# Attention and FFN in one kernel: heads in natural rows, three score buffers shared by two engines, score fills in twos

## Chip, cores, metric

One core of one Trainium2 chip. The metric is device time in microseconds of one execution. The profiled execution is one of a kernel's runs; its span is about 2 us shorter than the time that is reported for it. In the lines of profiles PE is TensorE, PEld its weight loads, DVE VectorE, ACT ScalarE and POOL GpSimd; x4 stands for four instructions merged into one line, and `<-PE ps` names what ended a wait.

## The reference

Batch 1, 2048 tokens, width 512, 32 heads of 16, FFN width 1792, bfloat16 inputs. The inputs' setup is left out.

```python
def reference(A_x, A_wqkv, A_wo, B_x, B_w1, B_w3, B_w2):
    x = A_x
    xn = _layernorm(x)                                   # no gain, no bias
    qkv = (xn @ A_wqkv).reshape(B, S, 3, 32, 16) ...     # q, k, v per head
    p = softmax(einsum("bhqd,bhkd->bhqk", q, k) * 0.25)
    a = einsum("bhqk,bhkd->bhqd", p, v) ... @ A_wo
    h = silu(xn @ B_w1) * (xn @ B_w3)
    return x + a + h @ B_w2
```

## The kernel before

The kernel is laid out ahead of time by a small scheduler in Python: it keeps a model clock for each engine, and at each step hands TensorE the next piece of work by priority. What runs on the chip is the fixed order of instructions that comes out, with semaphores between the engines. A "pair" below is one pair of PSUM banks with scores of two heads, 128 keys by 512 queries each. There are 1024 pairs. ScalarE turns a pair into exponentials with one instruction ("exp"); VectorE does it with "p1" on a pair and four further instructions for every two pairs, by integer arithmetic on bfloat16 bits. The weighted sums of V ("PV"), the FFN and the output projections are TensorE's other work; its last part of the FFN, h times w2, is called w2 here.

Scores use 32 rows of the array for each head, so a head's 16 numbers of K and Q are spread over the 16 even rows of their group by a DMA through a staging tile, and the rest is filled with a constant that adds the bias of the exponent:

```python
        def pack(dst, keys, dkeys, scale, halves=(0, 1)):
            def evac(bk, o, rel):
                def emit():                                  # PSUM -> stg on VectorE (scaled for Q)
                    ...
                    for hh in halves:
                        P.post("sp", lambda hh=hh: moves(hh), ready=q.end + _LAT, prio=1)
                def moves(hh):
                    m = P.dma(lambda e: e.dma_start(dst(hh), stg[64 * hh:64 * hh + 64, sl, :]), ...)
```

The constant is put there by ScalarE (first group) and by POOL (the others). The score buffers are private: banks 0–3 are two pairs for ScalarE, banks 4–5 one pair for VectorE. Scores for ScalarE go first:

```python
        def try_a():                      # a pair for ScalarE
            bufs = [0]
            if idle((2, 3)):
                bufs = [0, 1]
            ...
            x = score(2 * buf, "A", *nx)
        def try_d():                      # a pair for VectorE
            if st["pos"] >= NR or st["early"] or not idle((4, 5)) or dbuf[0] > P.t:
                return False
            x = score(4, "D", *nx)
        ...
                    elif try_a() or try_d() or (... try_dense() ... try_pv() ... try_dense()):
```

`early` is the prologue: as long as it lasts, banks 4–6 belong to the projections and VectorE gets no scores. All 16 copies of V for all heads, 512 columns each, lie in that phase.

## Time and profile before

| | before |
|---|---|
| time, median of the first 3 runs | 813.42 us (812.09 to 815.43) |
| span of the profiled run | 812.3 us |
| exps on ScalarE / p1 on VectorE | 794 / 230 |
| first exp, first p1 | 19.1 us, 48.9 us |
| 100th pair, 1000th pair begun | 105.0 us, 774.0 us |
| from the 1000th pair to the end | 38.3 us |

The last two rows cut the span into three lengths: a **head** (to the 100th pair: 105.0 us), a **middle** of 900 pairs (669.0 us) and a **rest** (38.3 us). A pair counts as begun when its exp or p1 starts; the times are read off the single records of the trace. Such marks are better than idle columns here, since the records of successive exps overlap.

ScalarE's timeline of the kernel before (start, length, engine, line, instruction, and in brackets the idle time ahead with what ended it):

```profile
7.67 1.09 ACT L1391 ACTIVATE f_xnT<-ps 128x512 bf16<-128x512 bf16 x2 [1.29 <-PE ps L1384]
10.56 1.09 ACT L1391 ACTIVATE f_xnT<-ps 128x512 bf16<-128x512 bf16 x2 [1.81 <-PE ps L1384]
14.01 0.60 ACT L1391 ACTIVATE f_xnT<-ps 128x512 bf16<-128x512 bf16 x1 [2.35 <-PE ps L1384]
18.12 1.09 ACT L1391 ACTIVATE f_xnT<-ps 128x512 bf16<-128x512 bf16 x2 [3.52 <-PE ps L1384]
19.10 1.95 ACT L1788 ACTIVATE f_PT<-ps 128x1024 bf16<-128x1024 f32 x2
```

ScalarE has waited 9 us in four gaps for transposed tokens by the time of its first exp, and the copies at 14.01 and 18.12 us are of later tokens than the first scores need.

### The profile page before, as it was taken

The numbers are of one execution on the slowest core, as the hardware profiler recorded it, in microseconds if no ns is written. First come the engines' busy times: TensorE is split into PE (matmuls) and PEld (weight loads), VectorE is DVE, ScalarE is ACT, GpSimd is POOL, SyncE is SP. The second block draws the span as 40 slices with busy tenths as digits, with TensorE's granted clock in tenths as the row PEclk, the third lists the DMA queues.
The fourth block names the chain that finished last, engine by engine and source line by source line (L and its number), as shares of the span: only waits on it lengthen the run. The fifth ranks groups of instructions, "written<-read, shape, count | busy, mean of one in ns | idle before, by whom it ended". The sixth has DMA issues, their size and how long they took to land.

```text
span 812.3 us, 20816 instructions
## 1 busy us (share of the span) xinstructions
PE 775.6 (95%) x8925; PEld 224.6 (28%) x8925; DVE 775.1 (95%) x1015; ACT 776.0 (96%) x874; POOL 44.1 (5%) x54
## 2 busy tenths in 40 slices
PE   6999999999999999999999999999999999999987
PEld 4332222222222222222222222222222222222222
DVE  8679999999999999999999999999999999999982
ACT  4899999999999999999999999999999999999992
POOL 4500100000000000000001000000000000000000
PEclk9999999999999999999999999999999999999997
DMA  5216333233222313333112434321223432222211
GB/s 182 54 31 149 49 49 52 45 54 40 29 22 41 49 38 43 41 54 47 19 25 28 60 41 54 48 33 40 18 27 55 67 34 34 49 27 22 28 9 31
DMA packets 88783, 36.96 MB, mean 45 GB/s; under 512 B 73193, under 2 KB 85097, under 8 KB 88681
## 3 DMA queue, kind: packets, MB, share of 16 engines
q1 hardware_dynamic: 88680, 35.53, 29.9%
q8 instruction: 72, 1.18, 0.6%
q14 instruction: 31, 0.25, 0.1%
HBM read 22.81 MB, written 2.10 MB: 31 GB/s over the span
## 4 chain that ended last, share of the span: by engine, by line
ACT 50%; PE 24%; DVE 19%; DMA 3%; issue 2%; POOL 1%; SPq 1%; DVEq 0%; POOLq 0%
ACT f_PT L1788 48%; PE ps L1356 9%; PE ps L1742 8%; DVE f_xd L1837 6%; PE ps L2010 6%; ACT f_th L1517 3%; DVE f_xd L1900 3%; DVE f_xd L1909 2%; DVE f_xd L1950 2%; DVE f_xd L1893 2%; DMA f_R<-f_Rrow 2%; DMA f_Rrow<-f_Rc 1%; DVE f_hT L1531 1%; SPq L2058 1%; DVE f_t L1521 1%
## 5 line engine op out<-in xcount | busy, mean ns | idle before, releaser
L1788 ACT ACTIVATE f_PT<-ps 128x1024 bf16<-128x1024 f32 x794 | 746.4, 1091 | 9.9 <-PE ps L1742 9.1
L1742 PE MATMUL ps<-f_QT,f_KT 32*128 32x512 bf16 x2048 | 331.0, 385 | 14.1 <-ACT f_PT L1788 7.1
L1837 DVE TENSOR_SCALAR f_xd<-ps 128x1024 int16<-128x1024 f32 x230 | 278.6, 1211 | 1.6 <-PE ps L1742 1.2
L2010 PE MATMUL ps<-f_PT,f_Vaug 128*17 128x512 bf16 (+1 forms) x1588 | 211.0, 386 | 0.3 <-DVE f_xd L1900 0.3
L2010 PE MATMUL ps<-f_xd,f_Vaug 128*17 128x512 bf16 (+1 forms) x1380 | 191.5, 387 | 3.5 <-DVE f_xd L1950 2.6
L1742 PEld LDWEIGHTS ps<-f_QT,f_KT 32*128 32x128 bf16 x2048 | 83.5, 91 | 328.6 <-ACT f_PT L1788 277.2
L1356 PE MATMUL ps<-f_xnT,f_w 128*32 128x512 bf16 x1792 | 145.0, 384 | 2.5 <-DVE f_hT L1531 0.9
L1900 DVE TENSOR_TENSOR f_xd<-f_xd 128x2048 bf16<-128x2048 bf16 x115 | 142.1, 1235 | 0.0
L1909 DVE TENSOR_SCALAR f_xd<-f_xd 128x2048 int16<-128x2048 int16 x115 | 81.2, 706 | 0.0
L1893 DVE TENSOR_SCALAR f_xd<-f_xd 128x2048 int16<-128x2048 int16 x115 | 79.4, 691 | 0.6 <-PE ps L1356 0.2
L1950 DVE TENSOR_SCALAR f_xd<-f_xd 128x2048 int16<-128x2048 int16 x115 | 79.0, 687 | 0.0
L1356 PE MATMUL ps<-f_w,f_hT 128*32 128x512 bf16 x896 | 74.9, 384 | 0.0
L2010 PEld LDWEIGHTS ps<-f_PT,f_Vaug 128*17 128x17 bf16 (+1 forms) x1588 | 50.6, 92 | 54.4 <-issue 44.7
L2010 PEld LDWEIGHTS ps<-f_xd,f_Vaug 128*17 128x17 bf16 (+1 forms) x1380 | 46.2, 92 | 54.7 <-issue 30.4
L2075 POOL TENSOR_TENSOR f_onorm<-f_U,f_R 128x512 bf16<-128x512 f32 x15 | 21.5, 1431 | 705.2 <-DMA f_R<-f_Rrow 549.3
L1356 PEld LDWEIGHTS ps<-f_xnT,f_w 128*32 128x32 bf16 x1792 | 36.6, 94 | 64.9 <-issue 56.5
L1517 ACT ACTIVATE f_th<-ps 128x512 f32<-128x512 f32 x56 | 38.7, 691 | 0.0
L1531 DVE SCALAR_TENSOR_TENSOR f_hT<-f_t,ps 128x512 bf16<-128x512 bf16 x56 | 37.8, 675 | 0.7 <-PE ps L1356 0.5
L1521 DVE SCALAR_TENSOR_TENSOR f_t<-f_th,ps 128x512 bf16<-128x512 f32 x56 | 37.7, 674 | 0.5 <-ACT f_th L1517 0.3
L1356 PEld LDWEIGHTS ps<-f_w,f_hT 128*32 128x32 bf16 x896 | 18.6, 94 | 26.8 <-issue 22.4
L1356 PE MATMUL ps<-f_wo,f_onorm 128*32 128x512 bf16 x272 | 22.2, 401 | 1.9 <-POOL f_onorm L2075 1.8
L2028 DVE COPY f_U<-ps 128x512 f32<-128x512 f32 x31 | 21.1, 679 | 0.4 <-PE ps L2010 0.3
(80 smaller groups left out, 240.6 us busy)
## 6 DMA issues: line engine op xcount, KB each, us to landing
f_w<-in_B_w_dram SPq DMA_DIRECT2D x112, 128.0 KB, 2.7
f_R<-f_Rrow SPq DMA_DIRECT2D x124, 32.0 KB, 4.4
f_xr<-in_A_x_dram SPq DMA_DIRECT2D x16, 128.0 KB, 3.8
out_dram<-f_xn_sb SPq DMA_DIRECT2D x16, 128.0 KB, 2.5
f_KT<-f_stg SPq DMA_DIRECT2D x31, 64.0 KB, 2.0
f_QT<-f_stg SPq DMA_DIRECT2D x31, 64.0 KB, 2.0
f_U<-f_U SPq DMA_DIRECT2D x60, 32.0 KB, 1.9
f_w<-in_B_w_dram SPq DMA_DIRECT2D x7, 256.0 KB
```

The source lines that it names most:

```text
L1356: ins = e.matmul(bank(bk)[32 * i:32 * i + 32, 0:ncols], make_lhsT(i), rhs_ap, start=start, stop=stop, tile_position=(0, 32 * i))
L1517: q = P.op("act", lambda e: e.activation(th[:, ss, :], bank(bk), ACTF.Tanh, scale=0.5), reads=[("ps", bk)], writes=[("th", ss)], dur=a_cos ...
L1521: q2 = P.op("dve", lambda e: e.scalar_tensor_tensor(t1[:, ss, :], th[:, ss, :], 1.0, bank(bk), ALU.add, ALU.mult), reads=[("th", ss), ("ps ...
L1531: q = P.op("dve", lambda e: e.scalar_tensor_tensor(hT[:, fc, :], t1[:, ss, :], 0.5, bank(bk), ALU.mult, ALU.mult), reads=[("t1", ss), ("ps ...
L1742: ins = e.matmul(bank(b), l_, r_, start=True, stop=True, tile_position=(rp, 0))
L1788: q = P.op("act", lambda e: e.activation(PT[:, s_, :], ps[:, b0 * 512:(b0 + 2) * 512], ACTF.Exp, scale=ASC, bias=ABIAS), reads=[("ps", b0) ...
L1837: q = P.op("dve", lambda e: e.tensor_scalar(dsl[:, ys, 1024 * c:1024 * c + 1024], ps[:, 4 * 512:6 * 512], G_LO, 32767.0, ALU.max, ALU.min) ...
L1893: P.op("dve", lambda e: e.tensor_scalar(dsl[:, NY + m_, 0:n], y, 0x7F, 0x3F00, ALU.bitwise_and, ALU.bitwise_or), reads=YK, writes=[("ds", ...
L1900: q_ = P.op("dve", lambda e: e.tensor_tensor(t_ap.bitcast(BF16), y.bitcast(BF16), t_ap.bitcast(BF16), ALU.mult), reads=YK + [("ds", NY + m ...
L1909: q_ = P.op("dve", lambda e: e.tensor_scalar(g_ap, y, -G_LO, 0.0, ALU.add, ALU.max), reads=YK, writes=[("g", g_, k) for k in range(n // 51 ...
L1950: q_ = P.op("dve", lambda e: e.tensor_scalar(y, y, 0x7F80, None, ALU.bitwise_and), reads=YK, writes=YK, dur=s_cost(n), name="e", lock=True)
L2010: ins = e.matmul(bank(PV)[32 * j:32 * j + (17 if g % 2 == 0 else 32), :], v_, p_, start=s0, stop=s1, tile_position=(0, 32 * j))
```

## The change

The intent: (1) K and Q stay in the rows in which the projection delivers them, two heads in each group of 32 rows; Q is kept in two copies, each masked to one of the two heads, so that the other head's 16 rows multiply by zero. Staging DMAs and constant fills go; the bias moves into p1. (2) The first projections are done token tile by token tile, with dummy matmuls put in to keep the array warm, and their copies are shared by ScalarE and VectorE; V for heads 0 to 7 is packed by fours into 4 copies, and the other 16 copies of V move out of the prologue. (3) The three pairs of score banks are shared by both engines; where two are free, TensorE fills both, on opposite row groups, before it turns to column work. (4) PV groups may wait longer for more members. The core of the diff (cut; "..." marks cuts, and the comments in it are added here):

```diff
-    NPR = 10
+    NPR = 12
-    PVQ = 20
+    PVQ = 28
+    A_SOON = 0.7
+    D_SOON = 0.6
+    VB0 = 24
+    VBS = 5
-    ABIAS = -127.0 * math.log(2.0) + math.log(KAPPA)
+    ABIAS = math.log(KAPPA)
...
-        def kt_fill(g):                       # POOL fills of K with the constant
...
@@ tile_QT
+                    q = P.op("dve", lambda e: e.tensor_scalar(QT[:, s1, :], bank(bk), QS, None, ALU.mult), ...)
+                    q = P.op("dve", lambda e: e.tensor_scalar(QT[:, s0, :], QT[:, s1, :], msk[:, 0:1], None, ALU.mult), ...)
+                    q = P.op("dve", lambda e: e.tensor_scalar(QT[:, s1, :], QT[:, s1, :], msk[:, 1:2], None, ALU.mult), ...)
...
+        for t in range(NT):                   # V of heads 8 to 31, out of the prologue
+            crit.append((VB0 + VBS * t, k, tile_VB(t)))
...
+        def open_bufs():
+            bs = [0]
+            if idle((2, 3)):
+                bs.append(1)
+            if not st["early"] and idle((4, 5)):
+                bs.append(2)
+            return [b_ for b_ in bs if pbuf[b_] <= P.t + A_EARLY]
 
         def try_a():
...
+            two = len(free) > 1
+            if not two and not st["early"]:   # one free buffer: fill it alone only when it is due
+                due = max(P.t, P.free["act"]) + 0.905 * st["wait_a"] - A_SOON
+                if due > P.t and sorted(pbuf)[1] <= due + A_OVER:
+                    return False
+            if not one_a(free[0], ...):
+                return False
+            if two and not st["early"]:
+                one_a(free[1], st["last_par"])
...
         def try_d():
-            if st["pos"] >= NR or st["early"] or not idle((4, 5)) or dbuf[0] > P.t:
+            if st["pos"] >= NR or st["early"] or st["hold_d"] or not d_due():
...
-                                                          G_LO, 32767.0, ALU.max, ALU.min),
+                                                          YB, G_LO, ALU.add, ALU.max),
...
-            if len(pick) < 4 and not closed and P.t - oldest < 1.2:
+            if len(pick) < 4 and not closed and P.t - oldest < 2:
...
-                    elif try_a() or try_d() or (...
+                    elif try_d() or try_a() or (...
```

## The prediction

> **What bounds the kernel now.** I read the page's busy shares first, then the same engines stage by stage, then the groups of instructions, then a few microseconds of the timeline, and last the start times of single records in the trace. Busy shares and stages:
>
> ```profile
> PE 775.6 (95%) x8925; PEld 224.6 (28%) x8925; DVE 775.1 (95%) x1015; ACT 776.0 (96%) x874; POOL 44.1 (5%) x54
> ...
> 0.00:20.00 20.00, 12.84 (x126) 8.54 (x126) 16.22 (x42) 8.91 (x13) 8.56 (x20) 1.00 0.58 184
> 20.00:40.00 20.00, 18.12 (x280) 7.83 (x284) 14.04 (x30) 17.64 (x24) 11.48 (x12) 1.00 0.24 55
> 40.00:60.00 20.00, 19.78 (x264) 6.40 (x256) 15.42 (x20) 18.27 (x21) 0.00 (x0) 1.00 0.11 27
> 60.00:780.00 720.00, 701.17 (x8026) 194.11 (x8024) 714.67 (x902) 715.36 (x802) 24.05 (x22) 1.00 0.31 43
> ```
>
> (columns of the stages: PE, weight load, DVE, ACT, POOL busy, clock, DMA share, GB/s.) From 60 to 780 us three engines are all over 97% busy. There are 1024 pairs of score banks; ScalarE turns 794 of them into exponentials (L1788), VectorE 230 (L1837 and a chain of four operations per two pairs). The pairs are dealt out between the two, so their joint rate sets the end, and TensorE fills the banks for both:
>
> ```profile
> L1788 ACT ACTIVATE f_PT<-ps 128x1024 bf16<-128x1024 f32 x794 | 746.4, 1091 | 9.9 <-PE ps L1742 9.1
> L1742 PE MATMUL ps<-f_QT,f_KT 32*128 32x512 bf16 x2048 | 331.0, 385 | 14.1 <-ACT f_PT L1788 7.1
> L1837 DVE TENSOR_SCALAR f_xd<-ps 128x1024 int16<-128x1024 f32 x230 | 278.6, 1211 | 1.6 <-PE ps L1742 1.2
> L1900 DVE TENSOR_TENSOR f_xd<-f_xd 128x2048 bf16<-128x2048 bf16 x115 | 142.1, 1235 | 0.0
> L1909 DVE TENSOR_SCALAR f_xd<-f_xd 128x2048 int16<-128x2048 int16 x115 | 81.2, 706 | 0.0
> ```
>
> The idle column suggests that almost nothing is lost (9.9 us on ScalarE). It misleads: records of successive exps overlap (mean 1091 ns), so a short wait is hidden in the overlap. Start to start in the trace, a fed exp takes 904 ns (half of them 904 or 905), but the 744 exps that start between 60 and 780 us average 930 ns: **19 us lost on ScalarE**. In 129 gaps with over 30 ns lost, 16.6 us together, nearly every exp starts 0.43 us after a score matmul starts: it waited for that matmul. The same count for VectorE (p1 1.134, multiply 1.133, the three others 0.60 each when fed) gives **17 us lost**, about 9 of it beside the 1.43 us normalisations on POOL (L2075).
>
> Why is TensorE late? The timeline:
>
> ```profile
> 401.77 0.12 PEld L1742 LDWEIGHTS ps<-f_QT,f_KT 32*128 32x128 bf16 x4 [0.42 <-ACT f_PT L1788]
> 401.78 0.41 PE L1742 MATMUL ps<-f_QT,f_KT 32*128 32x512 bf16 x4
> 402.12 0.10 PEld L2010 LDWEIGHTS ps<-f_PT,f_Vaug 128*32 128x32 bf16 x4 [0.23 <-issue]
> 402.12 0.40 PE L2010 MATMUL ps<-f_PT,f_Vaug 128*32 128x512 bf16 x4
> ...
> 402.45 0.10 PEld L1742 LDWEIGHTS ps<-f_QT,f_KT 32*128 32x128 bf16 x2 [0.23 <-ACT f_PT L1788]
> 402.45 0.39 PE L1742 MATMUL ps<-f_QT,f_KT 32*128 32x512 bf16 x2
> 402.77 0.12 PEld L1356 LDWEIGHTS ps<-f_w,f_hT 128*32 128x32 bf16 x8 [0.23 <-issue]
> 402.77 0.61 PE L1356 MATMUL ps<-f_w,f_hT 128*32 128x512 bf16 x8
> ```
>
> Score matmuls use 32 rows of the array ("row"), all others 32 columns ("col"). Row to col and col to row take 0.32 us start to start (medians 318 and 322 ns), col to col 0.216; a second pair on the other two row groups (the x4 at 401.78) costs almost nothing. Between 60 and 780 us I count 738 row stretches, 520 with one pair, 206 with two, 12 with three, and 1616 col groups, of which 166 PV groups hold two matmuls where four fit. The sum, 738 x 0.64 + 878 x 0.217 + 33 between row groups, is 695 us of 720: TensorE is truly full, though its score loads show 277 us of waits for ScalarE.
>
> **What the Trainium skill says.** "TensorEngine Tiling (Array Packing)", Key Properties: changing the tiling mode drains TensorE, while different tiles can run in parallel. The trace agrees: 0.32 against 0.216 us, and four row groups together. "SBUF — State Buffer", Who interferes with whom: a VectorE instruction in a 2-port mode and a GpSimd one lock each other out for a whole instruction. The trace agrees, and it costs the prologue dearly:
>
> ```profile
> 7.82 1.90 POOL L1275 TENSOR_SCALAR f_KT<-f_pat 128x2048 int16<-128x2048 int16 x1
> 7.88 2.30 DVE L1242 TENSOR_SCALAR f_xn_sb<-f_xd,f_mv,f_lnr 128x512 bf16<-128x512 bf16 x2 [0.59 <-POOL f_lnr L1230]
> ```
>
> Two such normalisations take 0.70 us elsewhere, 2.30 beside the POOL fill. "TensorE: Matmul & The Clock Gate", The HAM clock gate: cold matmuls of 128 columns run at about 107 ns, warm ones at 56, and idling makes it cold again. The 40 warming matmuls here took 4.45 us (111 each), and the first projections at 14.3 us still ran 0.43 us apart, twice the later 0.216. "VectorE: DVE Perf Modes", tier table: tensor_scalar on 16-bit SBUF data reaches 4x. The 2048-wide ones here take 0.60 us start to start, which agrees.
>
> **The change part by part.**
> *Row stretches.* Three buffers shared, two filled at once on opposite row groups. If the 966 pairs of the middle come in about 580 stretches rather than 738, TensorE saves 158 x (0.64 - 0.217) = 67 us. Fuller PV groups: some 80 groups fewer, 17 us. V for heads 8 to 31 moves from the prologue into the run: 64 groups, 14 us back. TensorE falls to about 86 to 90% of the middle: no longer a bound, but single fills stay whenever VectorE holds one of three buffers (p1 alone reads 1.13 us of each 3.2 us).
> *ScalarE in the middle.* It loses 19 us; I let it keep 6. (720 - 27 for 56 tanh - 6)/0.904 = 760 exps instead of 744.
> *VectorE in the middle.* A pair costs 1.134 + (1.133 + 3 x 0.60)/2 = 2.60 us; 222 pairs, 17 us lost, so 126 us of other work. Added: two mask multiplies for each of 15 Q tiles; between the 0.15 us that the 2048-wide rate gives and the 0.32 us of L1242, I estimate 0.25 each, 7.5 us. I let the losses fall from 17 to 12, as the POOL normalisations stay. (720 - 126 - 7.5 - 12)/2.60 = 221 pairs. Together 981 against 966 pairs, 1.6% more: **-11 us**.
> *The added YB, the bias and the missing clamp* leave element counts alike: 0. The staging DMAs that go were hidden: 0.
> *Prologue.* Now the first exp starts at 19.1 us, the first p1 at 48.9, and 35 + 5 pairs have begun by 60 us. The POOL fills of K (11 us, one on the path: 1.6) go; the first projections are done tile by tile on a warm array with evacuations on both engines, and the next transposes no longer stand in front of them. First exp, estimated: about 12 us. The early phase needs 4 V evacuations instead of 16 and no second K and Q tile, so it can end when VectorE has normalised all x tiles: 12 tiles at about 1.05 us, plus some 6 us of copies, from 11 us, is about 30. Pairs by 60 us: 14 exps before 30 (two in 2.5 us, as now), 32 after, 5 or 6 by VectorE beside 16 V copies of 0.46 us and the next K and Q: 52. Twelve ahead, at the present pace of 916 pairs in 680 us (0.74 us each): **-9 us**.
> *Tail.* The same structure: 0, with a doubt of 3 us (its clock halves at 789 us, 0.54 in the stage 790 to 800).
> Sum: 813.4 - 11 - 9 = about **794 us**.
>
> **The rivals.**
> *A: the losses do not move.* Sharing three buffers, VectorE takes one for the wait, the fill and p1, and ScalarE is back on two; the kernel fills a lone buffer only when the next exps are about 0.7 us off, little over 0.32 + 0.43. For it: the just-in-time rule; against: the freed array and the 40% of the time with three. ScalarE keeps 15 us, the middle gains 2 to 3, the time is 802 to 805.
> *B: VectorE starves instead.* Its buffer is now asked for only 0.6 us before it is free, where before it had its own. For it: p1 must follow in order; against: scores for VectorE go first and the chain offers other work. 5% of VectorE lost (36 us) is 10 to 14 pairs: about 800 to 803.
> *C: both engines run full and the prologue gains more* (first exp at 11, early phase over by 25 us): ScalarE loses 3 us, 16 pairs ahead at the start: 785 to 788.
> *D: the array goes cold in the middle, or the saturation test of the int16 conversion fails and the slow plan runs as well.* Nothing in the trace speaks for it: between 20 and 40 us, with PE 91% busy, the clock is 1.00. It would cost tens of us to a doubling; 2% at most.
>
> **Range and chances.** The two terms, 11 and 9, are each uncertain by about 5 and partly go together, which gives 783 to 804. 2% faster is below 797.2, inside the range but on the good side of the middle: 0.67. Within 2%: 0.31. Slower: 0.02, from D.
>
> **What would show it.** Right: about 550 to 620 row stretches between 60 and 780 us, over half with two pairs; exps there at most 912 ns apart on average; PE busy below 95%; first exp at 11 to 13 us, first p1 near 30; no POOL instruction beside the first norms; 50 or more pairs begun by 60 us; mask multiplies of 0.2 to 0.3 us. Wrong: exps still 925 ns or more apart (A), gaps before p1 that name L1742 (B), a first exp after 15 us, or a tail over 30 us after the last full stretch of exps.

## More of the kernel before

The stages of the middle of the kernel before (columns: stage, length, busy time and number of instructions of PE, weight load, DVE, ACT, POOL; clock; DMA share; GB/s):

```profile
60.00:300.00 240.00, 234.31 (x2670) 65.28 (x2668) 238.36 (x303) 239.32 (x268) 8.97 (x12) 1.00 0.34 52
300.00:500.00 200.00, 192.28 (x2214) 53.48 (x2212) 197.48 (x249) 197.30 (x222) 6.72 (x4) 1.00 0.30 40
500.00:700.00 200.00, 195.60 (x2236) 54.01 (x2232) 199.15 (x252) 199.10 (x226) 5.81 (x4) 1.00 0.32 42
700.00:780.00 80.00, 78.98 (x916) 21.34 (x914) 79.68 (x102) 79.64 (x89) 2.55 (x2) 1.00 0.23 25
```

The kernel is full on three engines alike in every stage; none stands out as slack that another could use.

## The result

Before 814.25 us (median of 4, 812.09 to 815.43), changed 800.50 us (median of 4, 800.16 to 801.96). Ratios are the mean time of one kernel's runs over that of the other's of the same rounds, so not quite the ratio of the medians: 0.9838, with a 95% interval of 0.9811 to 0.9864. That is 1.6% less time: inside the range on record, 6 us above the predicted time, and counted as "same" at the bar of 2%. A second measurement of the unchanged kernel (`after_again`, below) gave 0.9824.

Cut into the three lengths, the profiled runs say where the 13.9 us of the spans come from, and it is not where the prediction had them:

| | head | middle (900 pairs) | rest | span |
|---|---|---|---|---|
| before | 105.0 | 669.0 | 38.3 | 812.3 |
| changed | 92.1 | 672.2 | 34.1 | 798.4 |
| difference | **-12.9** | **+3.2** | **-4.2** | -13.9 |
| predicted | -9 | -11 (over 966 pairs) | 0 | about -20 |

**Head.** ScalarE's timeline of the changed kernel, to be read against that of before:

```profile
7.42 1.09 ACT L1347 ACTIVATE f_xnT<-ps 128x512 bf16<-128x512 bf16 x2 [5.34 <-PE ps L1340]
8.74 1.09 ACT L1347 ACTIVATE f_xnT<-ps 128x512 bf16<-128x512 bf16 x2 [0.24 <-PE ps L1340]
9.96 0.49 ACT L1381 ACTIVATE f_KT<-ps 128x384 bf16<-128x384 f32 x1
10.40 1.05 ACT L1399 ACTIVATE f_QT<-ps,f_mskq 128x384 bf16<-128x384 f32 x2
11.94 1.02 ACT L1837 ACTIVATE f_PT<-ps 128x1024 bf16<-128x1024 f32 x1 [0.48 <-PE ps L1774]
```

and VectorE's:

```profile
7.84 0.74 DVE L1239 TENSOR_SCALAR f_xn_sb<-f_xd,f_mv,f_lnr 128x512 bf16<-128x512 bf16 x2 [0.59 <-POOL f_lnr L1227]
...
32.02 1.23 DVE L1909 TENSOR_SCALAR f_xd<-ps 128x1024 int16<-128x1024 f32 x1 [0.54 <-PE ps L1774]
```

The second pair of normalisations is 0.74 us where it was 2.30; from the last transposed copies that the first scores need (8.74; before 10.56) to the first exp it is 3.2 us instead of 8.5; and VectorE joins at 32.0 us instead of 48.9. By 60 us, 56 pairs have begun instead of 40.

**Middle.** The stages of the changed kernel:

```profile
60.00:300.00 240.00, 229.94 (x2740) 64.56 (x2740) 234.76 (x306) 239.68 (x270) 9.05 (x9) 1.00 0.29 39
300.00:500.00 200.00, 189.44 (x2236) 52.08 (x2230) 196.87 (x252) 198.86 (x226) 5.84 (x4) 1.00 0.29 39
500.00:700.00 200.00, 191.03 (x2242) 52.90 (x2242) 197.41 (x254) 199.29 (x226) 5.61 (x4) 1.00 0.29 39
```

ScalarE is a little fuller, VectorE a little emptier, TensorE 95% busy, not the 86 to 90% of the prediction. The groups of the changed kernel's page show the same exchange:

```profile
PE 754.4 (94%) x9157; PEld 222.4 (28%) x9157; DVE 766.3 (96%) x1032; ACT 774.9 (97%) x876; POOL 32.8 (4%) x45
...
L1837 ACT ACTIVATE f_PT<-ps 128x1024 bf16<-128x1024 f32 x801 | 751.7, 1155 | 4.8 <-PE ps L1774 2.7
L1774 PE MATMUL ps<-f_QT,f_KT 32*128 32x512 bf16 x2048 | 313.4, 385 | 25.8 <-ACT f_PT L1837 17.8
L1909 DVE TENSOR_SCALAR f_xd<-ps 128x1024 int16<-128x1024 f32 x223 | 271.5, 1218 | 4.8 <-PE ps L1774 3.5
```

The idle time ahead of exps fell from 9.9 to 4.8 us; that ahead of p1 rose from 1.6 to 4.8, 3.5 of it named as waiting for the score matmul. ScalarE takes 801 pairs and VectorE 223: seven pairs changed hands. Counted start to start as in the prediction (the changed kernel's middle from 60 to 770 us, since its work thins out earlier; a row stretch is a run of score matmuls between two pieces of column work):

| | before, 60–780 us | predicted | changed, 60–770 us |
|---|---|---|---|
| score ("row") stretches | 738 | about 580 | 697 |
| of these with one pair / two / three or more | 520 / 206 / 12 | over half with two | 457 / 227 / 13 |
| column groups per us | 2.24 | fewer | 2.26 |
| mean distance of exps | 930 ns | at most 912 | 923 ns |
| lost on ScalarE | 19 us | 6 | 14 |
| lost on VectorE | 17 us | 12 | 26 |
| pairs per us | 1.342 | 1.36 | 1.338 |

A few microseconds of TensorE's timeline of the changed kernel:

```profile
402.05 0.39 PE L1774 MATMUL ps<-f_QT,f_KT 32*128 32x512 bf16 x2
...
402.92 0.39 PE L1774 MATMUL ps<-f_QT,f_KT 32*128 32x512 bf16 x4
...
403.79 0.39 PE L1774 MATMUL ps<-f_QT,f_KT 32*128 32x512 bf16 x2
...
404.66 0.39 PE L1774 MATMUL ps<-f_QT,f_KT 32*128 32x512 bf16 x2
```

x4 is a stretch with two pairs, x2 one with a single pair. Most are still single: every 0.87 us or so TensorE goes back for one pair, at 0.32 us each way, as before.

**Rest.** 34.1 against 38.3 us. In the kernel before, the granted clock was half from 788.9 to 799.1 us of the trace; in the changed one from 780.0 to 783.4, in each of them apart from the last 3.0 and 1.4 us of the span.

### The profile page after: what moved, and what is told of

Its sections match the earlier page's. It is cut to its first block, busy times and chain, and to the rows that moved or that the text cites. A ratio compares the mean times of both kernels' runs of the same rounds, so it can differ in the third digit from the quotient of the medians.

```text
span 798.4 us, 21147 instructions
## 1 busy us (share of the span) xinstructions
PE 754.4 (94%) x9157; PEld 222.4 (28%) x9157; DVE 766.3 (96%) x1032; ACT 774.9 (97%) x876; POOL 32.8 (4%) x45
## 4 chain that ended last, share of the span: by engine, by line
ACT 65%; DVE 18%; PE 14%; issue 1%; DMA 1%; POOL 0%; SPq 0%; DVEq 0%
ACT f_PT L1837 62%; DVE f_xd L1909 5%; PE ps L1328 5%; PE ps L1774 4%; PE ps L2027 4%; DVE f_xd L1958 3%; ACT f_th L1542 3%; DVE f_xd L1951 2%; DVE f_xd L1973 1%; DVE f_xd L1967 1%; DVE f_t L1546 1%; DVE f_hT L1556 1%; DVE f_stats L1252 1%; DMA f_R<-f_Rrow 1%; DVE f_U L2045 0%
## 5 line engine op out<-in xcount | busy, mean ns | idle before, releaser
L1774 PE MATMUL ps<-f_QT,f_KT 32*128 32x512 bf16 x2048 | 313.4, 385 | 25.8 <-ACT f_PT L1837 17.8
L1909 DVE TENSOR_SCALAR f_xd<-ps 128x1024 int16<-128x1024 f32 x223 | 271.5, 1218 | 4.8 <-PE ps L1774 3.5
L2027 PE MATMUL ps<-f_xd,f_Vaug 128*17 128x512 bf16 (+1 forms) x1338 | 185.8, 385 | 4.3 <-DVE f_U L2045 1.8
L1774 PEld LDWEIGHTS ps<-f_QT,f_KT 32*128 32x128 bf16 x2048 | 78.8, 91 | 332.7 <-ACT f_PT L1837 272.1
L1328 PE MATMUL ps<-f_xnT,f_w 128*32 128x512 bf16 x1792 | 140.6, 384 | 3.9 <-DVE f_t L1546 3.2
L1958 DVE TENSOR_TENSOR f_xd<-f_xd 128x2048 bf16<-128x2048 bf16 x112 | 138.2, 1234 | 0.0
L1951 DVE TENSOR_SCALAR f_xd<-f_xd 128x2048 int16<-128x2048 int16 x112 | 78.2, 698 | 2.2 <-PE ps L2027 1.6
L1973 DVE TENSOR_SCALAR f_xd<-f_xd 128x2048 int16<-128x2048 int16 x112 | 80.1, 715 | 0.0
L1967 DVE TENSOR_SCALAR f_xd<-f_xd 128x2048 int16<-128x2048 int16 x112 | 76.5, 683 | 0.0
L1542 ACT ACTIVATE f_th<-ps 128x512 f32<-128x512 f32 x56 | 41.4, 739 | 0.0
L1328 PE MATMUL ps<-f_wo,f_onorm 128*32 128x512 bf16 x272 | 21.6, 387 | 0.8 <-DVE f_wkv L1599 0.4
```

The source lines that it names most:

```text
L1328: ins = e.matmul(bank(bk)[32 * i:32 * i + 32, 0:ncols], make_lhsT(i), rhs_ap, start=start, stop=stop, tile_position=(0, 32 * i))
L1542: q = P.op("act", lambda e: e.activation(th[:, ss, :], bank(bk), ACTF.Tanh, scale=0.5), reads=[("ps", bk)], writes=[("th", ss)], dur=a_cos ...
L1774: ins = e.matmul(bank(b), l_, r_, start=True, stop=True, tile_position=(rp, 0))
L1909: q = P.op("dve", lambda e: e.tensor_scalar(dsl[:, ys, 1024 * c:1024 * c + 1024], ps[:, b0 * 512:b0 * 512 + 1024], YB, G_LO, ALU.add, ALU. ...
L1951: P.op("dve", lambda e: e.tensor_scalar(dsl[:, NY + m_, 0:n], y, 0x7F, 0x3F00, ALU.bitwise_and, ALU.bitwise_or), reads=YK, writes=[("ds", ...
L1958: q_ = P.op("dve", lambda e: e.tensor_tensor(t_ap.bitcast(BF16), y.bitcast(BF16), t_ap.bitcast(BF16), ALU.mult), reads=YK + [("ds", NY + m ...
```

## The experiments

All kernels but one (`nomask`, said there) computed results within the tolerance. "h / m / r" are head, middle and rest of the profiled run, as above; "ratio" is against the kernel before in the same rounds on the same chip. The kernel before measured 814.2, 816.2 and 815.7 us (medians of 11) beside the three groups of runs.

### layout: the change without the sharing and the double filling

The changed kernel, with `try_a`, `try_d` and their choice of pairs put back to private buffers:

```diff
-        pbuf = [0.0] * 3
+        abuf = [0.0, 0.0]
+        dbuf = [0.0]
...          (open_bufs, d_due, one_a out; try_a, try_d, a_next, d_next as before)
-                    elif try_d() or try_a() or (...
+                    elif try_a() or try_d() or (...
```

> The changed kernel with the filling rules of before: two bank pairs for ScalarE and one for VectorE, one filled at a time, the order of tries of before. Kept: natural rows, masked Q, new prologue, split V tiles, 12 P slots, the longer PV wait. Theory P (the prologue made the gain: 56 pairs begun by 60 us against 40, 16 x 0.74 us = 12 us): 801 to 803 us, all but 1 or 2 us of the gain. Theory S (the shared buffers made it, and the head start is paid back in the middle by the mask multiplies and the V work moved there): 809 to 812 us, with 56 or 57 pairs by 60 us all the same, and exps in the middle 928 ns or more apart.

Measured: 806.11 us (803.64 to 807.89), ratio 0.9894 [0.9865, 0.9923]; h / m / r 91.5 / 670.1 / 40.3. That is between what theory P gave (801 to 803) and what theory S gave (809 to 812): neither holds as it stands. The head is all there without the sharing; so is the pace of the middle, which is 1 to 2 us shorter than with it, although its clock was half for 3.4 us. VectorE loses 13 us between the 100th and the 980th pair instead of 23. Its p1 waits less, too (group line of this kernel, against the 4.8 of the changed one):

```profile
L1863 DVE TENSOR_SCALAR f_xd<-ps 128x1024 int16<-128x1024 f32 x227 | 276.3, 1217 | 2.4 <-PE ps L1768 1.9
```

But 6 us are given back in the rest. TensorE's timeline of this kernel after its last score matmul, at 780.91 us:

```profile
784.28 1.44 PE L1328 MATMUL ps<-f_w,f_hT 128*32 128x512 bf16 x14
...
786.64 0.83 PE L1328 MATMUL ps<-f_w,f_hT 128*32 128x512 bf16 x12
...
788.38 1.48 PE L1328 MATMUL ps<-f_w,f_hT 128*32 128x512 bf16 x24
```

f_w from f_hT is w2: 56 of its matmuls (these 50 and three twos between PV groups) are still to be done when the last scores are out. In the changed kernel none is; what comes there is only the output projection, f_wo:

```profile
787.26 0.83 PE L1328 MATMUL ps<-f_wo,f_onorm 128*32 128x512 bf16 x12
...
789.00 1.91 PE L1328 MATMUL ps<-f_wo,f_onorm 128*32 128x512 bf16 x32
```

So the sharing is worth something (0.9894 against 0.9838 and 0.9824, about 5 us, the intervals just miss each other), and not by a faster middle. That it works by freeing TensorE for the end is what `single`, `single_light` and `layout_trim` test. A scheduler that hands out w2 earlier with private buffers would be the other test; it was not run.

### b_shared: the sharing and double filling alone

The kernel before, with the changed kernel's `open_bufs`, `try_a`, `one_a`, `d_due`, `try_d` and order; layout, prologue and PV groups as before.

```diff
-        abuf = [0.0, 0.0]
-        dbuf = [0.0]
+        pbuf = [0.0] * 3
...          (try_a, try_d, a_next, d_next as in the changed kernel)
-                    elif try_a() or try_d() or (...
+                    elif try_d() or try_a() or (...
```

> The kernel before with the changed filling rules alone: three shared bank pairs, filled two at a time, VectorE's buffer asked for late; interleaved heads, DMA staging, old prologue and old PV wait stay. Theory P: 811 to 813 us, as before. Theory S: 805 to 807 us, exps between 60 and 780 us at most 918 ns apart, VectorE losing no more than before (17 us).

Measured: 813.31 us, ratio 0.9979 [0.9949, 1.0009]; 104.1 / 667.8 / 36.9. Theory P (811 to 813) fits and theory S (805 to 807) does not. Where the head stays at its old length, the sharing gains about 2 us, and the interval includes none. It makes ScalarE lose 14 instead of 18 us and VectorE 22 instead of 16: the exchange that the changed kernel shows, without its new layout. Row stretches between the 100th and the 980th pair are 647 (before 673, changed 645): the sharing with double filling does all the little that is done about them. The run also bears on the main question. The page of this kernel:

```profile
PE 758.7 (94%) x8913; PEld 217.6 (27%) x8913; DVE 771.5 (95%) x1008; ACT 775.2 (96%) x877; POOL 42.4 (5%) x54
```

TensorE is busy 17 us less than in the kernel before (775.6), with nearly the same matmuls (8913 and 8925); 13.5 us of it lie in the middle, which is 1.2 us shorter. Time saved on TensorE did not turn into pairs here. The test isn't clean, though: ScalarE did lose 4 us less, and whether the sharing took back on VectorE what a freer TensorE gave to ScalarE can't be told apart in this run.

### single: the sharing without the second fill

```diff
             if not one_a(free[0], ...):
                 return False
-            if two and not st["early"]:
-                one_a(free[1], st["last_par"])
             return True
```

> The changed kernel without the second fill of a try (three shared buffers, each filled by itself when its turn comes). If filling two at a time is what frees TensorE, row stretches in the middle rise from 697 towards 730 or more and the time by 3 us or more; if the shared pool itself is what helps and the pairs meet anyhow, the middle keeps its pace (exps within 3 ns of 923 apart) and the time moves by at most 2 us, apart from the tail.

Measured: 809.56 us, ratio 0.9935 [0.9904, 0.9965]; 94.8 / 671.8 / 43.2. The middle is as long as the changed kernel's, with 667 stretches instead of 645; the rest is 9 us longer. TensorE's timeline of this kernel after the last score matmul (785.80 us) shows why:

```profile
787.64 1.25 PE L1328 MATMUL ps<-f_w,f_hT 128*32 128x512 bf16 x20
788.82 1.05 PE L2112 MATMUL ps<-f_sell,f_U 128*128 128x4 f32 x8
...
791.55 5.79 PE L1328 MATMUL ps<-f_w,f_hT 128*32 128x512 bf16 x104
```

136 matmuls of w2 are left over, 104 of them in one stretch of 5.8 us. The size fits: 22 row stretches more at 0.64 - 0.22 us are 9 us of TensorE, and 136 matmuls, four at a time at 0.22 us, are 7.5 us. It does so only roughly, for `layout`, with 19 stretches more (664), leaves 56 matmuls or 3 us.

### vearly: V put back into the prologue

```diff
-    VB0 = 24
-    VBS = 5
+    VB0 = 0
+    VBS = 0
```

> The changed kernel with the V tiles of heads 8 to 31 back in the early phase (due at position 0). Theory P: the early phase lasts until about 47 us again, the first p1 comes at 47 to 49 us, fewer than 47 pairs have begun by 60 us, and the time rises by 6 to 8 us to 807 to 809. If the head start is paid back later anyhow (theory S) the rise is at most 3 us.

Measured: 811.18 us, ratio 0.9946 [0.9916, 0.9976]; 102.0 / 670.4 / 37.0. The first exp is at 11.8 us as in the changed kernel, but the first p1 is at 45.8 (changed: 32.0), and 45 pairs instead of 56 have begun by 60 us, about as theory P had it; the time rose by 9 to 10 us where it gave 6 to 8. Of the head's gain of 12.9 us, 9.9 are gone when V is put back, and only some 3 are left for everything that brings the first exp forward. (What moving V alone gains in the kernel before was not run.) VectorE's timeline of this kernel:

```profile
38.43 0.56 DVE L1512 CAST f_Vaug<-ps 128x384 bf16<-128x384 f32 x1 [1.33 <-PE ps L1503]
40.45 1.21 DVE L1512 CAST f_Vaug<-ps 128x384 bf16<-128x384 f32 x2 [1.46 <-PE ps L1503]
45.76 1.22 DVE L1909 TENSOR_SCALAR f_xd<-ps 128x1024 int16<-128x1024 f32 x1
```

VectorE waits for V to be projected, and because the phase lasts, it has no score buffer to fill the gaps with. The rest is 3 us longer than the changed kernel's; the clock was half from 777 to 794 us in this run, so that part can't be laid on V.

### b_fill: the kernel before, its first POOL fill moved out of the way

```diff
-            P.post("pool", lambda g=g: kt_fill(g), ready=8.0 if g == 1 else 26.0 + 2 * g, prio=3)
+            P.post("pool", lambda g=g: kt_fill(g), ready=11.0 if g == 1 else 26.0 + 2 * g, prio=3)
```

> The kernel before with the POOL fill of the second K half moved from 8 to 11 us, so that it does not stand beside the normalisations of x tiles 2 and 3. Theory: those two take 0.7 us and not 2.3, the first exp comes 1.5 to 3 us earlier than 19.1 and the time falls by 1 to 2 us (812 to 813). Rival: the first scores still stand behind the transposes of tiles 4 and 5, so the first exp stays at 18.5 to 19.1 and nothing changes.

Measured: 813.81 us, ratio 0.9973 [0.9952, 0.9993]; 104.5 / 666.7 / 37.8. The normalisations at 7.9 us took 0.74 us instead of 2.30, but the fill came down on the next ones instead (2.29 us at 13.30), and the first exp moved from 19.1 to 18.5 us only. The test did not take the clash away, it moved it; it shows that 1.6 us at that one place are worth about half a microsecond at the head, and leaves the first exp where the rival put it (18.5 to 19.1). The time fell by 2 us all the same, as the theory had it (the interval gives 0.6 to 3.9); but the profiled middle, far from that fill, is 2.3 us shorter, so most of it can't be put down to the clash.

### light: half of w2 left out

If a fuller TensorE sets the losses, then taking work away must give the exps their time back. The changed kernel with 7 of w2's 14 groups, some 24 us of TensorE (the result is still within the tolerance, although half of a product is missing; it is no kernel to use):

```diff
-                    [("hT", fc), ("w2", fc)], None) for fc in range(FC)]
+                    [("hT", fc), ("w2", fc)], None) for fc in range(0, FC, 2)]
```

> The changed kernel with every second w2 group left out (wrong result on purpose). Nothing of w2 is left after its last score matmul as it is. Theory L: TensorE does not pace the exps any more, so 24 us less of its work change the time by at most 2 us (798.5 to 802). Rival B (TensorE is still the bound of the middle): ScalarE's loss falls from 13 to under 8 us, VectorE's from 23 to under 15, and the time to 794 or less.

Measured: 812.73 us, ratio 0.9961 [0.994, 0.9983]; 92.5 / 680.6 / 37.5. Less work made the kernel 12 us **slower**; neither theory foresaw that. Two things are to be read. First, where less work met a full clock, the pairs came no faster: from the 300th to the 600th pair (243 to 470 us, 243 to 465 in the changed kernel) TensorE was 94% busy instead of 96%, yet it took 226.5 us instead of 221.4. The test is weaker than it was meant to be, since the scheduler pulled the remaining dense work forward and TensorE stayed nearly as full as long as there was any. Of the 5 us, 2.5 are a wait of VectorE at 396 us for the DMA of x (`f_xr`), which the changed kernel doesn't have; the rest stays open. Second, the clock. The stages of this kernel (PEclk is the third figure from the end):

```profile
690.00:710.00 20.00, 17.25 (x162) 4.74 (x164) 19.56 (x24) 20.00 (x23) 0.95 (x1) 1.00 0.22 15
710.00:724.00 14.00, 13.22 (x90) 2.43 (x90) 11.18 (x15) 11.20 (x13) 0.79 (x1) 0.51 0.00 1
...
758.00:778.00 20.00, 19.43 (x124) 3.44 (x120) 17.88 (x24) 17.73 (x19) 1.27 (x1) 0.50 0.05 3
```

The last w2 matmul was done at 689 us. From then on TensorE had only scores and PV: 162 matmuls in 20 us (the changed kernel: 2242 in 200 us, 224 in 20), 86% busy, and the clock was taken to half in stretches of 13.7, 13.7, 20.5 and 3.4 us. At half the clock a score matmul takes 0.60 us instead of 0.39, and ScalarE waits for it (timelines of PE and of ACT):

```profile
759.01 0.60 PE L1774 MATMUL ps<-f_QT,f_KT 32*128 32x512 bf16 x2
```

```profile
760.73 1.02 ACT L1837 ACTIVATE f_PT<-ps 128x1024 bf16<-128x1024 f32 x1 [0.53 <-PE ps L1774]
762.23 3.77 ACT L1837 ACTIVATE f_PT<-ps 128x1024 bf16<-128x1024 f32 x4 [0.48 <-PE ps L1774]
```

So the dense work, w2 as the last of it, seems to be the filler that keeps the array at full clock: in nine of the fourteen traces, `light` and both main kernels among them, a half-clock stretch begins 6 to 21 us after the last w2 matmul, well before the end. It isn't the only condition: in eight traces the clock was also half for 3.4 or 6.8 us long before w2 ended, among them `layout` (740 us), `nomask` (75 and 375), `dsoon12` (516) and `cost` (504); what set those off was not tested.

### single_light: single, with half of w2 left out

Both edits above together. It asks whether the leftover of w2 is what makes `single` slow.

> The run 'single' (shared buffers, each filled by itself) with every second w2 group of the output tiles left out: wrong result on purpose, 112 col groups or 24 us of TensorE time less, nothing changed for ScalarE or VectorE. Theory L (TensorE's total work is a bound that shows only at the end: in 'single' 136 of the w2 matmuls run after the last score matmul): no w2 matmul is left after the last score, the stretch from the last exp to the end falls from 23.6 to about 15 us and the time from 809.6 to 800 to 802. Rival M (single fills slow the exps themselves): no shorter than 806.

Measured: 812.12 us, ratio 0.9956 [0.9933, 0.998]; 95.2 / 676.6 / 35.5. The rest does shrink by 7.7 us, from 43.2 to 35.5, to about that of the changed kernel, and no w2 is left over: that half of the explanation holds. The time does not follow (800 to 802 expected): w2 ended at 717 us, from 731 us on the clock was half for 27 us before the last 1 us of the span, and the middle is 5 us longer. The clock muddies this experiment, so `layout_trim` below takes less away.

### nomask: no second and third operation on Q

Wrong result (both heads of a row group read the same, unmasked Q; relative error 1.19), to price the masks:

```diff
-                    q = P.op("dve", lambda e: e.tensor_scalar(QT[:, s0, :], QT[:, s1, :], msk[:, 0:1], ...
-                    q = P.op("dve", lambda e: e.tensor_scalar(QT[:, s1, :], QT[:, s1, :], msk[:, 1:2], ...
+            uq = (u - u % 2) % 4           # both heads read the slot of the first
```

> The changed kernel without the two mask multiplies of a Q tile: one copy serves both heads' groups (wrong result on purpose). VectorE saves 1.29 - 0.60 = 0.69 us for each of 15 tiles, 10 us, which is 4 pairs at 2.6 us, or 3 us of the end: 797 to 798.5. If VectorE's waits are set by the order of its work and not by its amount, 800 to 802.

Measured: 797.93 us (795.65 to 799.89), ratio 0.9763 [0.974, 0.9786]; 93.4 / 670.6 / 34.0. Against the changed kernel's two ratios this is 0.6 to 0.75% less, 5 to 6 us with a doubt of 3. The profiled run, the slowest of its five, shows only 1 to 2 us of it in the middle, where its clock was half for 3.4 us. VectorE loses as much as with the masks (24 us). So the masks are not what makes VectorE lose time; they cost what they take. The groups of the changed kernel:

```profile
L1456 DVE TENSOR_SCALAR f_QT<-ps 128x512 bf16<-128x512 f32 x15 | 10.2, 683 | 2.4 <-PE ps L1328 2.4
L1459 DVE TENSOR_SCALAR f_QT<-f_QT,f_msk 128x512 bf16<-128x512 bf16 x15 | 5.3, 353 | 0.5
L1462 DVE TENSOR_SCALAR f_QT<-f_QT,f_msk 128x512 bf16<-128x512 bf16 x15 | 5.2, 348 | 0.0
```

Start to start they take 0.71, 0.27 and 0.26 us, where the single copy of before took 0.60: 0.64 us more for each of 15 tiles, 10 us instead of the 7.5 of the prediction (without the multiplies, in this run, the same copy takes 0.60). The multiplies were sized right (0.25); the copy ahead of them takes 0.11 us more than one whose result isn't read by the next instruction.

### after_again: the changed kernel once more

No edit.

> The changed kernel once more, unchanged, so that the other runs of this call have it on their chip: a ratio of 0.981 to 0.987 to the kernel before, and in its trace again about 56 pairs by 60 us, 13 us lost on ScalarE and 23 on VectorE between the 100th and the 980th pair, and 14 to 16 us from the last exp to the end. If the losses or the tail come out otherwise by more than 3 us, single traces can't carry such differences.

Measured: 800.98 us (799.5 to 802.08), ratio 0.9824 [0.98, 0.9848]; 92.0 / 671.4 / 34.3. The three lengths repeat within a microsecond.

### layout_trim: layout, without half of w2 in the last quarter of the queries only

```diff
-                    [("hT", fc), ("w2", fc)], None) for fc in range(FC)]
+                    [("hT", fc), ("w2", fc)], None) for fc in (range(FC) if qc < NQC - 1 else range(0, FC, 2))]
```

(with the edits of `layout`; result within the tolerance, not a kernel to use)

> The run 'layout' (private bank pairs) with every second w2 group of the last four output tiles left out: 28 groups, 6 us of TensorE time, wrong result in principle. Theory L (what 'layout' lacks against the changed kernel is TensorE time, and it shows as 56 w2 matmuls after the last score): no w2 matmul after the last score, a tail of 15 to 16 us and not 20.5, a time 4 to 6 us below 'layout', level with the changed kernel (within 2 us). Rival (the private banks pace the exps more slowly): still 4 us or more above the changed kernel of this call. A third way: the array runs out of work and goes to half clock before the end; then the clock record shows more than 10 us at 0.5.

Measured: 803.97 us (802.0 to 806.44), ratio 0.9864 [0.9838, 0.9891]; 91.7 / 670.8 / 38.6. The leftover is gone (last w2 matmul at 769.9 us), and from the last pair begun to the end it takes 16.1 us instead of 20.5. The time is 3 us above the changed kernel's, where theory L gave at most 2 and the rival at least 4. The ratio lies between those of `layout` and of the changed kernel, and overlaps both. The clock was half for 10.2 us from 777 us on in the profiled run, as in the kernel before. So the leftover of w2 accounts for a part of what the sharing is worth (1.7 us by the rest, 4.4 us from the last pair on); whether for all of it can't be told at a different clock and with intervals that overlap.

### dsoon12: VectorE asks for its buffer earlier

```diff
-    D_SOON = 0.6
-    D_RIDE = 1.0
+    D_SOON = 1.2
+    D_RIDE = 1.4
```

> The changed kernel with VectorE's buffer asked for 1.2 us (1.4 riding on a row stretch) before VectorE is free in place of 0.6 (1.0). If asking late is what makes VectorE lose 23 us in the middle where the private bank loses 13, the loss falls to 17 or less, with some more on ScalarE, and the time moves by -3 to 0 us. If the loss comes from the order of the work, VectorE's loss stays at 21 to 25 us and the time within 2 us or above.

Measured: 801.9 us, ratio 0.9839 [0.9806, 0.9871]; 93.4 / 672.6 / 33.8. VectorE loses 21.6 us instead of 22 to 23, ScalarE 15.1 instead of 13: nothing is won. By the mark set beforehand (17 us or less) asking too late is rejected as the reason, as far as 1.2 us of notice can show it.

### cost: the scheduler told the measured durations of the Q operations

```diff
-                             ... dur=d_cost(512), name="evQ")
+                             ... dur=0.712, name="evQ")
-                             ... dur=s_cost(512), name="evQ", lock=True)
+                             ... dur=0.268, name="evQ", lock=True)      # and 0.262
```

> The changed kernel planned with the measured durations of the three operations of a Q tile (0.712, 0.268, 0.262 us in place of 0.597, 0.209, 0.209): other instruction order, same work. If the queues were written in an order that these wrong durations spoil, VectorE's loss in the middle falls by 4 us or more and the time by 2 or more; if not, all stays within 2 us, and what moves is the tail.

Measured: 803.35 us, ratio 0.9847 [0.9823, 0.9871]; 92.5 / 675.5 / 35.1. No better: VectorE loses 28 us, of which up to 2 us lie in 6.8 us at half clock from 504 us on. A plan with wrong durations for these three operations isn't the reason for its loss either. No variant that computes the whole result beat the changed kernel.

**The clock in these times.** Executions of one kernel differ in their mean granted clock, and their times go with it: over the 95 of all kernels but the two with half of w2 gone, 0.001 more of clock goes with about 0.48 us less. The kernel before stood at 0.977 to 0.991 beside the experiments (its profiled run at 0.992), the changed one at 0.993 to 0.997. Brought to 0.997 by that slope, the mean times are, as an estimate good to about 1 us: before 809, `b_shared` 809, `vearly` 806, `layout` 805, `layout_trim` 801, changed 800.5, `nomask` 798. So at an equal clock some 9 of the 14 us are left, and about 5 go with the clock; `b_shared` keeps next to nothing, the masks cost 2.5 us, near the 3 that were expected, the place of V is worth 6 us instead of 10, and the leftover of w2 makes up most of what `layout` lacks.

## Why the prediction was right, and where it was not

The time lay in the range because one term came out larger than predicted, another not at all, and a third that was put at 0 helped. That is in part luck: rivals A (802 to 805) and B (800 to 803), with other mechanisms, lie nearer to 800.5 than the 794 of the prediction.

**The prologue: right, and mis-sized by a third.** First exp about 12 us, first p1 about 30, 52 pairs by 60 us, -9 us. Measured: 11.9, 32.0, 56 pairs; 16 pairs ahead at 0.74 us each are 12 us, and the head is 12.9 us shorter. `layout` shows the same 13.5 us without any sharing. `vearly` shows which part of the mechanism carries most of it: 9.9 us depend on the V copies leaving the phase in which VectorE has no score buffer. The prediction had named both and had let the early phase end at 30 us, but it gave the two no weights, and it let 52 pairs come out where 56 did. The POOL fill beside the norms, which it called dear, is worth half a microsecond at the head as far as `b_fill` shows.

**The middle: the step that failed.** It is "If the 966 pairs of the middle come in about 580 stretches rather than 738". They came at a rate of 697 in 710 us, 4% fewer per microsecond instead of 21%; 457 of them still held one pair. Column groups did not become fewer either: those of PV with two matmuls fell from 166 to about 140, not by 80. With the prediction's own sum and its 33 us taken over, 697 x 0.64 + (1607 - 697) x 0.217 + 33 us is 676 of 710 us, 95%, which is what the stages show. The sum was also kind to itself: a stretch with two pairs takes 0.12 us more, on average, than one with a single pair (0.44 against 0.32 from the first score to the next column matmul), so 158 stretches fewer are worth some 48 us and not 67. The 580 was an assumption with no count behind it: that three shared buffers leave two free at once most of the time was what the change hoped for.

**The second half of that step isn't borne out either**: that TensorE time saved becomes exps. `b_shared` saves 13.5 us of TensorE in the middle for 1.2 us of its length; `layout` has TensorE busy for 649 us of its middle of 670, the changed kernel for 643 of 672. In all kernels but `cost` and the two with half of w2 gone, the 900 pairs took 667 to 673 us. So the length of the middle does not follow the sum of TensorE's work in these runs. That a saving on TensorE would count with VectorE's loss held still is not excluded, since the comparisons that saved it, `light` apart, also changed who holds the buffers. The wait moved: ScalarE's loss went from 18.1 to 13.4 us and VectorE's from 15.8 to 23.4 us (between the 100th and 980th pair). Of the rivals, A (ScalarE's losses don't move) was nearly true, 14 us against the 15 that it gave, and B (VectorE starves) was true in kind, 26 us against 36, and B's 800 to 803 us is where the time came out. C (the early phase over by 25 us) did not come, and D's cold array not in the middle of the changed kernel's trace (after the start the clock is half first at 780 us). The masks took 10 us of VectorE instead of 7.5: right in kind, a quarter short.

**The tail: 0 predicted, -4.2 us measured from the 1000th pair on**, of which -1.9 from the last pair begun (16.5 to 14.6). The clock was half for 3.4 us there instead of 10.2; that is consistent, and by the estimate above the clock is worth 2 to 3 us between the two profiled runs (0.992 and 0.997) and about 5 between typical ones, but no run isolates it.

**What the sharing seems to be for** the prediction had not seen. With 13 us of head start the last score comes 13.5 us earlier (781.6 instead of 795.1), and TensorE's dense work must be finished by then too, or it stands at the end alone. `layout` leaves 56 w2 matmuls, `single` 136, the changed kernel none; the rests are 40.3, 43.2 and 34.1 us. With the old head nothing is left over in the first place, and there the sharing gains about 2 us, if anything (`b_shared`). So the gain of about 5 us is one that the sharing has together with the head start; that it would be smaller without it is likely by these runs, but the intervals leave room.

**Open**: why VectorE loses some 10 us more with a shared pool. Neither the masks (`nomask`), nor the notice it gives (`dsoon12`), nor the wrong durations in the plan (`cost`) is the reason; the sharing with its rules as a whole is (`b_shared` 22 against 16 without it, the changed kernel 23 against 13 in `layout`). The gaps lie ahead of p1 and beside POOL's normalisations, but which decision of the scheduler makes them wasn't tried.

## What to carry to other kernels

When several engines are full, count for each how much work is left when the last critical item has been issued: a head start becomes time in full only if every other engine can finish earlier too (`layout` had all of it and kept some 5 us less). Look at what shuts an engine out of its main work in the prologue before polishing the path to the first instruction: here putting V back cost 9.9 of the 12.9 us. And work that "fills" TensorE isn't idle ballast: in `light`, with half of w2 gone, the granted clock was half for over 50 us and the kernel 12 us slower. Compare executions at like clocks before a few microseconds are given to an edit.

## What the Trainium skill lacked or had wrong

- "TensorE: Matmul & The Clock Gate", HAM oscillation, gives as the rule no gaps of over some 3.4 us on TensorE; A second HAM failure mode adds that frequent micro-idles between matmul groups make the clock oscillate, without a figure for how thin the work may be. In `light` the clock fell to half although TensorE was 86% busy in the 20 us ahead (162 matmuls; 2.75 us idle in all, the longest gap 0.53 us). The number of matmuls doesn't decide it alone: in the changed kernel the clock stayed up at 224 per 20 us, and in `dsoon12` it fell at 516 us after 20 us with 220. All half-clock stretches that ended before the run did are multiples of 3.4 us, as the page's window would have it.
- "TensorEngine Tiling (Array Packing)", Key Properties, says that a change of the tiling mode drains TensorE and not what that costs: 0.32 us start to start between 32-row and 32-column matmuls of 512 columns here, against 0.216 us between column groups; the same before and after.
- No page that I read gives the time of a VectorE copy out of PSUM whose result the next instruction reads: here a 128x512 copy took 0.71 us start to start with such a reader behind it and, at the same line in `nomask`, 0.60 us without. Whether it is the reading or the kind of the next instruction was not tested.
